# A long convolution with a routed expert layer on one core: another spacing of the indirect transfers in the plan, and new due times

## The chip, the cores and the metric

One core of a Trainium2 chip runs the kernel. The metric is the device time of one launch in microseconds (us), as the median of several runs of the same program. The engines are called PE (TensorE, matmuls), DVE (VectorE), ACT (ScalarE), POOL (GpSimd) and SP (SyncE). Here SP issues all the plain transfers, and POOL issues the indirect ones.

## The reference, cut to what matters

The first half convolves every sequence with one filter as long as the sequence. The second half sends each token to the best of eight experts.

```python
B, S, D = 8, 5696, 128            # the convolution: x (B, S, D), h (S, D)
Y = rfft(x, n=2*S, axis=1) * rfft(h, n=2*S, axis=0)[None]
y = irfft(Y, n=2*S, axis=1)[:, :S]

N, E, F = 45568, 8, 1024          # the expert layer, on y.reshape(N, D)
logits = x @ w_gate + modality_bias[modality_id]
e_idx  = argmax(logits, axis=1)
gate_w = softmax(logits)[arange(N), e_idx]
for e in range(E):
    mask = e_idx == e
    out[mask] = gate_w[mask, None] * (maximum(x[mask] @ w1[e], 0) @ w2[e])
```

## The kernel before

The transform of the convolution is cut into three passes of small matmuls with scratch tensors in device memory between them. The batch of eight is done in four groups of two (`g` = 0 to 3). `stage1` is the first pass, `stage23` multiplies by the filter in the middle, and `stage4` is the last pass together with the routing.

`stage4` goes through each group in seven chunks. For a chunk it computes the tokens (PE line 738 or 744), the logits, the best expert, and each token's place in that expert's list (`places`, DVE, which writes the tile `idx`). Then POOL sends the rows to their places: one indirect transfer for every 128 tokens (`dispatch`, line 852, `rows<-rt,idx`). There are 360 of these. A chunk's rows wait for them in the tiles `rt`, of which there are eight (`RTB`).

`experts` takes blocks of 512 tokens (256 in the last level) out of the lists: two matmuls with a ReLU between them (lines 970 to 972 and 986 to 988; `hh` on ACT at line 975 and `hl` on DVE at line 978 split each result into two parts), a turn, and the gate (DVE, line 998). Then one indirect transfer for every 128 tokens writes the result to the output (`scatter`, POOL, line 1002, `out<-of,mrt`). There are 370 of these. The first expert blocks run while later groups are still being transformed and routed; the rest run after the last dispatch.

Nothing of this stands in a fixed order of loops. Every piece is a `step` with a duration on each engine that could do it, its predecessors, the buffers that it takes and frees, and a due time. `Plan.run` plays the steps through once while the program is built, and writes the instructions of each engine in the order in which it started them there. The due times (in the table `AIMS`: knots for each stage and a lead for each kind of step) say which ready step goes first. On the chip each engine then works through its own list in order, waiting only for data and buffers; times of the plan are not in the program.

Some steps may go to either of two engines, whichever is free. For POOL those are the sum of products in `stage23` (`add`, lines 633 and 634, DVE or POOL), the rests of the splits (`low` line 640, `uu_low` line 730, lines 885 and 952) and the token numbers (`token`, line 751).

The indirect transfers have a rule of their own in the plan. A step with `lag` is an indirect transfer, 1.35 us of POOL by the plan's account. Two lines of `first` decide:

```python
apart = begun[-self.BURST[0]] + self.BURST[1 if now < AIMS["tiles"][0] else 2]
kept = now >= apart and any(r[2].lag for r in ready["POOL"])
```

`begun[-4]` is the start of the fourth indirect transfer back. Before `apart` no further one is started. While `kept` holds (a transfer is ready and may go), POOL leaves the shared steps alone. The plan's clock `now` starts at 0.0 (line 217), and the first knot of `AIMS["tiles"]` is -726 before and -550 in the change. `ROWS` is what one indirect transfer takes of the plan's transfer channel.

Of the kernel before, what the change touches and what calls it, by code (L numbers as in the profile page):

```python
# [48 lines left out]
XB = 3  # L49

AIMS = {
    "first": (None, (-605, -183, 366), (-196, 637, 137), (625, 1000, -127)),
    "over": ((-368, -101, 125), (-635, -1076, -1685), (-39, 134, -1968), (563, 670, 333)),
    "route": ((-515, -163, -633), (-1563, -310, -744), (-281, 229, 525), (795, 397, 1519)),
    "weights": (-858, 184),
    "tiles": (-726, -304, 140, 719, 198, 755, 716),
    "lead": {
# [18 lines left out]
        "experts.load": 98, "experts.load_w": -19, "experts.load_raw": -51, "experts.w_high": 137,  # L76
        "experts.w_low": -159, "experts.prep": 2, "experts.x_high": 238, "experts.x_low": -41,
        "experts.gemm1": -106, "experts.h_high": 45, "experts.h_low": -43, "experts.gemm2": 120,
        "experts.result": 10, "experts.turn": -82, "experts.gate": -153, "experts.scatter": -53,
    },  # L80
}
WP = 256
# [53 lines left out]
class Plan:  # L136
# [3 lines left out]
    SYNC = {"PE": 1.89, "DVE": 0.15, "ACT": 0.15, "POOL": 0.2, "SP": 0.1, "-": 0.0}  # L140
    LAND = 2.98
    RATE = 0.30e6
    ROWS = 58e3
    BURST = 4, 7.13, 4.97

    def __init__(self):
        self.steps = []
# [19 lines left out]
    def run(self):  # L167
# [5 lines left out]
        channel = woken = 0.0  # L173
        begun = [-100.0] * self.BURST[0]

# [22 lines left out]
        def first(e):  # L198
            nonlocal woken

            apart = begun[-self.BURST[0]] + self.BURST[1 if now < AIMS["tiles"][0] else 2]
            kept = now >= apart and any(r[2].lag for r in ready["POOL"])
# [18 lines left out]
        while True:  # L221
            for e in ready:
# [14 lines left out]
                if x.lag:  # L237
                    begun.append(now)
                    channel = max(channel, now) + self.ROWS / self.RATE
                if x.bytes:  # L240
# [954 lines left out]
```

## Time and profile before

| | before |
|---|---|
| median of 3 runs | 2449.81 us (2447.63 to 2453.53) |
| the profiled execution | 2456.72 us, of which its span is 2454.7 us |
| PE busy | 2144.5 us (87%) |
| DVE busy | 1481.0 us (60%) |
| ACT busy | 1178.3 us (48%) |
| POOL busy | 1189.2 us (48%) |
| mean granted clock of PE | 0.926 |

The span runs from the first to the last instruction. A busy share is the time in which an engine worked on an instruction, at whatever clock. The granted clock is 1.0 at full speed and 0.5 at the lower level.

### The profile page before, as it was taken

The numbers are of one execution on the slowest core, as the hardware profiler recorded it, in microseconds if no ns is written. First come the engines' busy times: TensorE is split into PE (matmuls) and PEld (weight loads), VectorE is DVE, ScalarE is ACT, GpSimd is POOL, SyncE is SP. The second block draws the span as 40 slices with busy tenths as digits, with TensorE's granted clock in tenths as the row PEclk, the third lists the DMA queues.
The fourth block names the chain that finished last, engine by engine and source line by source line (L and its number), as shares of the span: only waits on it lengthen the run. The fifth ranks groups of instructions, "written<-read, shape, count | busy, mean of one in ns | idle before, by whom it ended". The sixth has DMA issues, their size and how long they took to land.

```text
span 2454.7 us, 37648 instructions
## 1 busy us (share of the span) xinstructions
PE 2144.5 (87%) x11166; PEld 1779.7 (73%) x11166; DVE 1481.0 (60%) x2851; ACT 1178.3 (48%) x2392; POOL 1189.2 (48%) x1276
## 2 busy tenths in 40 slices
PE   5699878679775889999879889999788989999997
PEld 4578767557664667777767768887667768888897
DVE  5389645568333569975446679975354455555554
ACT  5556533335432456655445445565344344444443
POOL 2058543456445367854444566654445543333332
PEclk8899988889888999999988999999888999999999
DMA  8999887677765778964444435653323142121630
GB/s 290 292 311 322 262 260 232 219 236 234 238 183 181 221 236 260 302 226 160 145 144 142 141 106 171 203 176 105 97 72 121 58 116 74 48 78 44 248 104 26
DMA packets 236492, 434.69 MB, mean 177 GB/s; under 512 B 37318, under 2 KB 103850, under 8 KB 231681
## 3 DMA queue, kind: packets, MB, share of 16 engines
q1 hardware_dynamic: 212608, 384.15, 50.4%
q0 software_dynamic: 23680, 48.15, 5.8%
q8 instruction: 89, 1.46, 0.2%
q14 instruction: 115, 0.93, 0.1%
HBM read 408.11 MB, written 176.22 MB: 238 GB/s over the span
## 4 chain that ended last, share of the span: by engine, by line
PE 47%; issue 24%; POOL 7%; DMA 7%; another core or an unknown queue 6%; DVE 4%; ACT 2%; SPq 1%; POOLq 0%; ACTq 0%; DVEq 0%
PE bank L620 7%; POOL out L1002 4%; PE bank L972 3%; PE bank L970 3%; PE bank L552 3%; PE bank L986 3%; PE bank L971 3%; PE bank L744 3%; PE bank L987 3%; PE bank L988 3%; PE pl L763 2%; DMA zb<-z 2%; POOL rows L852 2%; DMA raw<-in_w 2%
## 5 line engine op out<-in xcount | busy, mean ns | idle before, releaser
L978 DVE SCALAR_TENSOR_TENSOR hl<-bank,hh 128x512 fp32r<-128x512 f32 x740 | 502.0, 687 | 384.8 <-ACT hh L975 239.5
L975 ACT ACTIVATE hh<-bank 128x512 fp32r<-128x512 f32 x740 | 439.3, 599 | 524.6 <-PE bank L972 309.4
L1002 POOL DMA_INDIRECT out<-of,mrt x370 | 369.0, 997 | 568.7 <-DVE of L998 425.7
L852 POOL DMA_INDIRECT rows<-rt,idx x360 | 358.7, 996 | 229.5 <-issue 127.7
L986 PE MATMUL bank<-hh,slot 128*128 128x512 f32 (+1 forms) x736 | 307.6, 418 | 22.0 <-ACT hh L975 10.9
L627 DVE TENSOR_TENSOR t<-bank,hs 96x512 f32<-96x512 f32 x418 | 264.7, 678 | 102.2 <-remote 40.0
L970 PE MATMUL bank<-mxh,slot 128*128 128x512 f32 (+1 forms) x736 | 308.2, 419 | 14.6 <-issue 8.8
L987 PE MATMUL bank<-hl,slot 128*128 128x512 f32 (+1 forms) x736 | 288.4, 392 | 2.8 <-DVE hl L978 1.7
L972 PE MATMUL bank<-mxh,slot 128*128 128x512 f32 (+1 forms) x736 | 287.7, 391 | 1.0 <-issue 1.0
L971 PE MATMUL bank<-mxl,slot 128*128 128x512 f32 (+1 forms) x736 | 287.9, 391 | 0.8 <-issue 0.7
L988 PE MATMUL bank<-hh,slot 128*128 128x512 f32 (+1 forms) x736 | 286.7, 390 | 0.6 <-issue 0.6
L620 PE MATMUL bank<-zb,m 96*96 96x256 f32 x896 | 236.3, 392 | 21.5 <-DMA zb<-z 10.8
L552 PE MATMUL bank<-xt,ft 128*128 128x256 f32 x540 | 151.8, 420 | 69.6 <-ACT z L445 27.2
L620 PEld LDWEIGHTS bank<-zb,m 96*96 96x96 f32 x896 | 146.7, 168 | 71.4 <-DVE hl L978 7.9
L445 ACT COPY ut<-bank 90x512 f32<-90x512 f32 x209 | 119.8, 581 | 132.2 <-remote 53.1
L633 POOL TENSOR_TENSOR t<-t,t 96x256 f32<-96x256 f32 x117 | 91.3, 781 | 188.7 <-DVE t L627 139.4
L986 PEld LDWEIGHTS bank<-hh,slot 128*128 128x128 f32 x736 | 143.1, 194 | 47.9 <-ACT hh L975 13.1
L970 PEld LDWEIGHTS bank<-mxh,slot 128*128 128x128 f32 x736 | 144.1, 196 | 43.9 <-issue 11.7
L552 PEld LDWEIGHTS bank<-xt,ft 128*128 128x128 f32 x540 | 108.7, 210 | 91.8 <-issue 32.0
L972 PEld LDWEIGHTS bank<-mxh,slot 128*128 128x128 f32 x736 | 142.9, 194 | 31.1 <-issue 0.8
L988 PEld LDWEIGHTS bank<-hh,slot 128*128 128x128 f32 x736 | 142.2, 193 | 29.7 <-issue 1.1
L987 PEld LDWEIGHTS bank<-hl,slot 128*128 128x128 f32 x736 | 143.1, 194 | 27.9 <-DVE hl L978 7.1
(226 smaller groups left out, 4110.3 us busy)
## 6 DMA issues: line engine op xcount, KB each, us to landing
slot<-weights SPq DMA_DIRECT2D x156, 1024.0 KB
z<-z SPq DMA_DIRECT2D x180, 256.0 KB
uu<-u SPq DMA_DIRECT2D x159, 256.0 KB
zb<-z SPq DMA_DIRECT2D x112, 360.0 KB
u<-ut SPq DMA_DIRECT2D x112, 360.0 KB
raw<-in_w SPq DMA_DIRECT2D x88, 256.0 KB
mrt<-rows SPq DMA_DIRECT2D x81, 260.0 KB
hs<-hd SPq DMA_DIRECT2D x96, 192.0 KB
```

Source lines behind the costliest of these rows:

```text
L552: nc.tensor.matmul(two(zt["ps"])[:, t], st["ft"][:, j, 2 * t:2 * t + 2, :], st["xt"][:, j], start=True, stop=True)
L620: nc.tensor.matmul(two(st["px"])[:KP, h], mm, both["zb"][:, k % 2, 1 - h], start=True, stop=True)
L852: nc.gpsimd.indirect_dma_start(views[count[0] % NVIEW], bass.IndirectOffsetOnAxis(ap=rs["idx"][:, t + c:t + c + 1], axis=0), st["rt"][:, c ...
L970: nc.tensor.matmul(po, w[0][:, fs], xh, start=True, stop=False)
L971: nc.tensor.matmul(po, w[0][:, fs], xl, start=False, stop=False)
L972: nc.tensor.matmul(po, w[1][:, fs], xh, start=False, stop=True)
L975: nc.scalar.activation(hf["hh"], hf["ph"], AF.Relu)
L978: nc.vector.scalar_tensor_tensor(hf["hl"], hf["ph"], 0.0, hf["hh"].bitcast(F32), op0=ALU.max, op1=ALU.subtract)
L986: nc.tensor.matmul(po, w[0][:, fs], hf["hh"][:, cs], start=k == 0, stop=False)
L987: nc.tensor.matmul(po, w[0][:, fs], hf["hl"][:, cs], start=False, stop=False)
L988: nc.tensor.matmul(po, w[1][:, fs], hf["hh"][:, cs], start=False, stop=k == 7)
L1002: nc.gpsimd.indirect_dma_start(oviews[(t * NSUB + c) % NVIEW], bass.IndirectOffsetOnAxis(ap=st["rt"].bitcast(I32)[:, c, D + 1:D + 2], axis=0),
```

## The change

The two gaps of `BURST`, the constant `ROWS`, and every number of `AIMS` are replaced. `AIMS["lead"]` gains entries for two kinds of steps, `fence` and `stage23.back`. No step is added or removed, and each engine's steps do the same work. The diff, with most of the table left out:

```diff
 AIMS = {
-    "first": (None, (-605, -183, 366), (-196, 637, 137), (625, 1000, -127)),
-    "over": ((-368, -101, 125), (-635, -1076, -1685), (-39, 134, -1968), (563, 670, 333)),
+    "first": (None, (-557, -190, 284), (-165, 620, 30), (608, 1003, -6)),
+    "over": ((-320, 32, 148), (-634, -1002, -1229), (148, 288, -2018), (456, 665, 85)),
...
-    "tiles": (-726, -304, 140, 719, 198, 755, 716),
+    "tiles": (-550, -95, 228, 735, -233, 786, 677),
...
-    ROWS = 58e3
-    BURST = 4, 7.13, 4.97
+    ROWS = 59e3
+    BURST = 4, 5.98, 7.06
```

The lists of POOL differ most. In both places below, a row is a line, an operation, the tile written and the tiles read, with their numbers, and how many of the same stand in a row. `L852` or `L853` (the change has one line more) are dispatches, `L1002` or `L1003` scatters.

The first place is in group 0, the dispatch of one chunk from the tiles `rt_1088` to `rt_1091`. Before:

```order
L852 DMA rows<-rt_1088,idx_1096 369152x130 x4
L852 DMA rows<-rt_1089,idx_1096 369152x130 x4
L852 DMA rows<-rt_1090,idx_1096 369152x130 x4
L852 DMA rows<-rt_1091,idx_1096 369152x130 x4
L751 COPY rt_1089<-tokid 128x4
```

With the change, the same chunk on POOL:

```order
L853 DMA rows<-rt_1088,idx_1096 369152x130 x4
L634 TENSOR_TENSOR t_1068<-t_1067,t_1068 96x256
L635 TENSOR_TENSOR t_1068<-t_1068,t_1067 96x256
L853 DMA rows<-rt_1089,idx_1096 369152x130 x4
L634 TENSOR_TENSOR t_1072<-t_1069,t_1072 96x256
L635 TENSOR_TENSOR t_1072<-t_1072,t_1069 96x256
L853 DMA rows<-rt_1090,idx_1096 369152x130 x4
L634 TENSOR_TENSOR t_1067<-t_1069,t_1067 96x256
L635 TENSOR_TENSOR t_1067<-t_1067,t_1069 96x256
L853 DMA rows<-rt_1091,idx_1096 369152x130 x4
```

One run of 16 transfers has become four runs of four, with one `add` of the other stage (two instructions) between each two.

The second place is late, in the last group, where dispatches and scatters alternate. Before, on POOL:

```order
L1002 DMA out<-of_2621,mrt_2606 45568x128 x4
L852 DMA rows<-rt_1091,idx_1096 369152x130 x3
L852 DMA rows<-rt_1090,idx_1096 369152x130 x3
L1002 DMA out<-of_2622,mrt_2607 45568x128 x4
L852 DMA rows<-rt_1090,idx_1096 369152x130
L852 DMA rows<-rt_1095,idx_1096 369152x130 x4
```

With the change, in the same part of POOL's list:

```order
L731 TENSOR_TENSOR uu_1081<-uu_1081 128x512
L853 DMA rows<-rt_1088,idx_1097 369152x130 x2
L1003 DMA out<-of_2638,mrt_2621 45568x128 x2
L752 COPY rt_1094<-tokid 128x4
L1003 DMA out<-of_2638,mrt_2621 45568x128 x2
L853 DMA rows<-rt_1088,idx_1097 369152x130 x2
L731 TENSOR_TENSOR uu_1080<-uu_1080 128x512
L853 DMA rows<-rt_1089,idx_1097 369152x130 x2
```

Here too at most four stand together, and what stands between two runs is by turns a split (line 730 before, 731 now) and a short copy of token numbers (751, now 752).

Counted over the whole list, up to the last dispatch: 45 unbroken runs of indirect transfers before, 119 now. Transfers that stand behind the eighth of their run, the last run of scatters alone left out: 280 before, 12 now. The last run, of scatters alone, has 196 transfers before and 220 now. On POOL there are 14 more `add` steps, 16 more of line 730, 16 fewer of line 640, 8 more of line 751, 4 more of line 885 and 4 fewer of line 952; the other engine that may do them has as many fewer or more. ACT takes 20 copies out of PSUM that DVE did.

## Rows read from the trace of the kernel before

**Rows 1.** Stretches: length, busy (count) of PE, PEld, DVE, ACT, POOL; clock, DMA, GB/s.

```profile
0.00:300.00 300.00, 241.74 (x1219) 200.56 (x1220) 202.86 (x324) 175.18 (x347) 139.16 (x179) 0.93 0.90 294
300.00:900.00 600.00, 476.85 (x2286) 383.94 (x2286) 304.31 (x752) 232.25 (x545) 289.83 (x315) 0.87 0.73 225
900.00:1140.00 240.00, 224.50 (x1182) 185.15 (x1180) 198.54 (x308) 147.06 (x295) 159.71 (x167) 0.96 0.79 248
1140.00:1490.00 350.00, 300.25 (x1566) 247.00 (x1565) 212.91 (x448) 164.69 (x342) 185.34 (x193) 0.90 0.45 136
1490.00:1715.00 225.00, 221.45 (x1216) 186.00 (x1215) 178.32 (x304) 128.51 (x248) 127.36 (x132) 0.99 0.54 166
1715.00:2000.00 285.00, 240.56 (x1144) 194.41 (x1143) 140.69 (x335) 116.65 (x238) 141.01 (x143) 0.89 0.30 87
2000.00:2300.00 300.00, 298.07 (x1379) 242.40 (x1378) 166.20 (x246) 144.75 (x246) 97.84 (x100) 0.99 0.28 91
```

**Rows 2.** The same stretches, instructions with tile idx alone: DVE, POOL (the dispatches).

```profile
300.00:900.00 600.00, 2.67 (x14) 179.68 (x180) 0.87 0.73 225
1140.00:1490.00 350.00, 1.27 (x7) 90.37 (x90) 0.90 0.45 136
1715.00:2000.00 285.00, 0.88 (x5) 80.77 (x82) 0.89 0.30 87
900.00:1140.00 240.00, 0.00 (x0) 0.00 (x0) 0.96 0.79 248
```

**Rows 3.** Timeline of POOL, one long run: start, duration, instruction, idle before it.

```profile
756.22 0.98 POOL L1002 DMA_INDIRECT out<-of,mrt  x1 [4.72 <-DVE of L998]
...
771.32 0.98 POOL L852 DMA_INDIRECT rows<-rt,idx  x1 [0.90 <-DVE sm L836]
...
793.46 0.98 POOL L852 DMA_INDIRECT rows<-rt,idx  x1 [0.30 <-issue]
```

**Rows 4.** The same run in stretches of 5 us, columns as in rows 1.

```profile
760.00:765.00 5.00, 5.00 (x28) 4.10 (x27) 0.52 (x2) 3.51 (x11) 3.78 (x5) 1.00 0.90 307
...
785.00:790.00 5.00, 0.00 (x0) 0.00 (x0) 0.00 (x0) 0.00 (x0) 3.78 (x5) 0.50 0.15 52
...
800.00:805.00 5.00, 5.00 (x16) 4.04 (x16) 0.00 (x0) 0.59 (x1) 0.00 (x0) 0.54 0.85 255
```

**Rows 5.** Timeline behind that run: the first ACT and PE work.

```profile
797.57 0.30 ACT L711 COPY gw<-gs 128x128 f32<-128x128 f32 x1 [16.65 <-remote]
...
799.08 2.08 PE L552 MATMUL bank<-xt,ft 128*128 128x256 f32 x4 [23.95 <-ACT z L445]
```

**Rows 6.** The run of 16 from 419.30 us, the first place of the order above.

```profile
425.00:430.00 5.00, 5.00 (x25) 3.97 (x24) 1.74 (x6) 0.59 (x1) 3.78 (x5) 1.00 0.44 155
430.00:435.00 5.00, 0.47 (x4) 0.16 (x2) 0.00 (x0) 0.00 (x0) 3.78 (x5) 0.76 0.50 137
435.00:440.00 5.00, 0.00 (x0) 0.00 (x0) 0.67 (x2) 0.00 (x0) 3.94 (x5) 0.50 0.26 92
```

**Rows 7.** Timeline of POOL: end of a run of 7, start of one of 13.

```profile
1323.13 0.98 POOL L852 DMA_INDIRECT rows<-rt,idx  x1 [0.30 <-issue]
1325.86 0.98 POOL L1002 DMA_INDIRECT out<-of,mrt  x1 [1.75 <-DVE of L998]
```

**Rows 8.** The first stretches of that run of 13, columns as in rows 1.

```profile
1326.00:1331.00 5.00, 5.00 (x31) 4.16 (x29) 5.00 (x11) 3.58 (x8) 3.78 (x4) 1.00 0.47 164
...
1336.00:1341.00 5.00, 2.44 (x11) 1.69 (x10) 1.29 (x2) 1.21 (x3) 3.92 (x4) 0.95 0.16 53
```

**Rows 9.** POOL's groups: count, busy us, mean ns, idle before them and what ended it.

```profile
L640 POOL TENSOR_TENSOR yl<-t,yh 96x512 fp32r<-96x512 f32 x76 | 99.8, 1319 | 63.4 <-ACT yh L637 57.8 <-PE bank L972 3.9 <-PE bank L988 1.4
...
L633 POOL TENSOR_TENSOR t<-t,t 96x256 f32<-96x256 f32 x117 | 91.3, 781 | 188.7 <-DVE t L627 139.4 <-DMA xt<-in_xq 40.4 <-PE bank L646 4.0
L730 POOL TENSOR_TENSOR uu<-uu 128x512 fp32r<-128x512 f32 x24 | 31.6, 1322 | 53.9 <-ACT uu L726 44.7 <-DVE yt L447 9.0
...
L751 POOL COPY rt<-tokid 128x4 int32<-128x4 int32 (+1 forms) x35 | 9.1, 278 | 0.0
```

More of the change, by code (lines that the diff above doesn't have):

```diff
@@ L51 @@
 AIMS = {
-    "first": (None, (-605, -183, 366), (-196, 637, 137), (625, 1000, -127)),
-    "over": ((-368, -101, 125), (-635, -1076, -1685), (-39, 134, -1968), (563, 670, 333)),
-    "route": ((-515, -163, -633), (-1563, -310, -744), (-281, 229, 525), (795, 397, 1519)),
-    "weights": (-858, 184),
-    "tiles": (-726, -304, 140, 719, 198, 755, 716),
-    "lead": {
[18 rows of a table removed]
[L76 to L79, printed above, removed]
+    "first": (None, (-557, -190, 284), (-165, 620, 30), (608, 1003, -6)),
+    "over": ((-320, 32, 148), (-634, -1002, -1229), (148, 288, -2018), (456, 665, 85)),
+    "route": ((-205, -198, -604), (-1533, -270, -708), (-571, 241, 527), (760, 399, 1189)),
+    "weights": (-781, 194),
+    "tiles": (-550, -95, 228, 735, -233, 786, 677),
+    "lead": {
[18 rows of a table added]
+        "fence": -108, "level.part": 21, "experts.load": 270, "experts.load_w": -54,
+        "experts.load_raw": -63, "experts.w_high": 179, "experts.w_low": -206, "experts.prep": -7,
+        "experts.x_high": 251, "experts.x_low": -11, "experts.gemm1": -160, "experts.h_high": 51,
+        "experts.h_low": -36, "experts.gemm2": 118, "experts.result": 133, "experts.turn": -88,
+        "experts.gate": -332, "experts.scatter": -44,
     },
```

36 rows, old and new, of the table AIMS are left out of this document.

## The prediction

> **What bounds the kernel now.** I read the busy time by stretch first [rows 1]. Take PE's busy time, times the granted clock, over the length of the stretch: the rate at which PE gets through its work, 1.0 at best. From 900 to 1140 us it is 224.50 x 0.96 / 240 = 0.90, from 1490 to 1715 us 221.45 x 0.99 / 225 = 0.97, and from 2000 us on 0.98. In three stretches it is lower: 476.85 x 0.87 / 600 = 0.69 from 300 to 900 us, 0.77 from 1140 to 1490 us and 0.75 from 1715 to 2000 us. No other engine is near its limit there: in the 600 us DVE works 304, ACT 232 and POOL 290. So PE waits in these stretches, and runs at a lower mean clock as well.
>
> The same stretches with only the instructions that read or write `idx` say what is special about them [rows 2]: they hold the dispatches, 180, 90 and 82 of the 360. The stretch at 0.90 has none.
>
> Then I looked at one long run of POOL. 29 indirect transfers begin at 756.22 us, and the last one begins at 793.46 us; but for one pause of 0.90 us they follow one another at 1.28 us [rows 3]. In the first 10 us PE loses nothing. From 785 to 790 us PE, ACT and DVE do nothing at all, while POOL goes on [rows 4]. The DMA engines are busy to 0.15 of their time then, so it is no lack of their time. ACT comes back at 797.57 us after 16.65 us idle, released by something that the profile does not name, and PE at 799.08 us after 23.95 us, waiting for ACT [rows 5]. Behind that PE has a clock of 0.54 for 5 us [rows 4]. The run of 16 at 419 us shows the same: ACT and DVE fall off between 425 and 430 us, PE between 430 and 435 us, at a clock that ends at the lower level, 0.50 [rows 6]. So POOL's run goes on unhurt, and about eight transfers into it the others stop.
>
> How short a run, or how long a pause, does no harm? Runs of four a tile apart, from 2000 to 2300 us, leave PE at 298 of 300 us [rows 1]. A run of 7, a pause of 1.75 us, and then a run of 13 [rows 7]: for 5 us behind that pause all three engines work well, and only 10 us into the second run PE loses half of its time [rows 8]. So 1.75 us between runs was enough there, while the 0.90 us inside the run of 29 did not prevent what came.
>
> **The change, part by part.** *The gap.* `now` starts at 0, and the first knot of `tiles` is negative before and after. So `now < AIMS["tiles"][0]` never holds, and the first of the two gaps is never used. Before, the plan asked for 4.97 us between a transfer and the fourth behind it; four of them take 4 x 1.35 = 5.4 us of the plan's POOL anyway, so there was no gap anywhere. Now it asks for 7.06 us in the whole program, a gap of 1.66 us behind each four. The "smaller one ahead of the experts", 5.98, does nothing.
>
> The gap itself is not in the program. What is there is the order: while the gap is open in the plan, `kept` is false and POOL may take a shared step. That is what the two places of the order show: an `add`, a split or a token copy behind each four. The transfers beyond the eighth of a run fall from 280 to 12, and these are the ones that see the others stop. On the chip the pause is as long as that step: an `add` is two instructions of about 0.78 us, 1.6 us in all, and the splits are 1.32 us, with an idle time ahead of them of 188.7 / 117 = 1.6 us for the first and 63.4 / 76 = 0.8 us for the one at line 640 [rows 9]. With it the pause is 2 to 3 us, over the 1.75 us above. A token copy gives 0.28 us, which is below the 0.90 us that was too short.
>
> *What it can give.* If the three stretches ran at the same 0.898, their work of 415, 270 and 214 us (busy time by clock, rows 1) would take 462, 301 and 239 us: 138, 49 and 46 less. The first cannot have all of it, because its transfers would have to fit: 0.73 x 600 = 438 us of DMA time. At the share of 0.90 of the first 300 us that takes 487 us, 113 less; at the 0.79 of the stretch at 0.90 it takes 554 us, 46 less. I take 80, the middle. The sum is 80 + 49 + 46 = 175 us. Of the late 46 us I keep half, 23: there the pause is by turns only a token copy. Of the other 129 us I keep 0.7, 90: the order all but ends the long runs, but a pause of 1.3 to 1.6 us lies close below the one that I know to be enough, where the step's data are ready. Together 113 us. The bounds are 0 (no pause is long enough) and 138 + 49 + 46 = 233 us (all of it, and the transfers keep up).
>
> In rows 4 ACT stops while nothing but POOL's transfers goes on. The Trainium skill's page "SBUF — State Buffer", section "Who interferes with whom", speaks against any such gain: transfers never contend with a compute engine, and PE and ACT never wait for anyone there. By that rule a run of transfers stops nothing, the term of 113 us is 0, and the sum is the 2450 us of before. The trace does not agree, as far as rows 4 go, and I give the rule the chance of rival three.
>
> *The moved work.* POOL gets 14 more `add` steps, 14 x 1.6 = 22 us. The 16 more of line 730 and the 16 fewer of line 640 cancel, at 1.32 us each [rows 9]; the rest are a few us. POOL is busy for 0.48 of the span and DVE is relieved, so I count nothing. Without that cover it would be the 22 us.
>
> *The due times.* They reorder all engines' lists. I see one thing in them that can be checked: the last run of scatters has 196 transfers before and 220 now, so 24 more come behind the last dispatch. From 2000 to 2300 us there were 100 [rows 1], 3.0 us each: 72 us more of expert work at the end, at full rate. It isn't a cost; it is work that no longer fills waits earlier. Where the rest moves a wait I can't tell, and I leave it at nothing, with rival two as its price.
>
> **The sum.** 2456.7 - 113 = 2343.6 us for a profiled execution. The one shown lies 6.9 us above the median of its runs, so 2336.7 us; I say 2337.
>
> **The rivals.**
>
> *One: the pauses are too short.* Four transfers, 5.1 us, and a step of 1.3 to 1.6 us stay below the 7.06 us that the plan asks for, and the trace has no case of many runs of four so close together. If a pause only delays the stop, a fifth of the 113 us is left: 2427 us. Against it stand rows 7 and 8, and the steps' own waits.
>
> *Two: slower, POOL's list becomes the bound.* POOL works in order. A shared step between two runs waits for its own data, and all transfers behind it wait too; then the eight `rt` tiles stay taken, and `stage4` on PE stops. For the first 180 dispatches the order has 11 runs before and 43 now, 32 more pauses, nearly all of them from 300 to 900 us. POOL is busy for 290 of the 600 us there, and the 0.30 us ahead of each of the 180 dispatches makes another 54 [rows 1 to 3]: 256 us are free. At the 1.6 us of rows 9 the new pauses take 51 of them. From 8 us each POOL is full; from 10.5 us each, (256 + 80) / 32, the loss is larger than the 80 us that the stretch may gain. At 12 us it is 48 us over that; the other two stretches give 0.7 x 49 + 23 = 57 us, and if half of that is lost in the same way, 28 us remain: 2450 + 48 - 28 = 2470 us. Waits of that kind exist: the first chain in rows 9 waits for DVE's products, which themselves wait for PE.
>
> *Three: no change, the runs are not the cause.* Dispatches come with chunks whose results everybody waits for; then the number of transfers, 730 as before, is what counts and not their spacing. That gives about 2450 us. For it: ACT's releaser in rows 5 is unnamed. Against it: the engines stop at the same place in the run in rows 4, 6 and 8, and none stops in the first 5 us. The Trainium skill's rule above, of the page "SBUF — State Buffer", would have it so.
>
> **How the numbers follow.** A difference of 0.2%, 4.9 us, is about what can be told from no change here. The forecast has a chance of 0.59, rival one 0.20, rival two 0.13, rival three 0.08. Faster are the forecast, most of rival one (0.17) and a little of rival three (0.02): 0.78. Same are 0.02 of rival one and 0.04 of rival three: 0.06. Slower are rival two and what is left of the others: 0.16. The forecast's own range is 2270 (all of the 175 us) to 2400 us (50 us gained). The range of 8 in 10 goes from 2255 us, a little below the 175 us towards the bound of 233, up to 2450 us: it leaves out rival two and the far tails.
>
> **What would show it.** Right: POOL's timeline has runs of four with a shared step between them; PE's waits of over 10 us between 300 and 900 us are gone; the rate of that stretch rises from 0.69 to about 0.8 with a DMA share of about 0.85; the mean clock rises above 0.93; and the last dispatch, before 2000 us until now, comes at about 2000 - 113 - 72 = 1815 us. Rival one: the same order, but ACT and DVE still idle in a series of runs. Rival two: POOL waits long at lines 634, 641 or 731, and PE for `rt`. Rival three: PE waits as long, at the same chunks, whatever the runs. What would make the forecast wrong above all is that the last two stretches keep their waits, because the short pauses of the late part stand behind those of 1140 to 1490 us as well.

## The result, and the profile after

The changed kernel takes 2284.57 us (median of 4 runs, 2280.05 to 2290.42). The kernel before, beside it on the same chip, took 2448.72 us (4 runs, 2438.36 to 2453.53). The ratio is 0.934, with a 95% interval of 0.930 to 0.938: 164 us faster, where 113 were forecast. The profiled execution took 2281.1 us with a span of 2279.3 us and a mean granted clock of 0.952. PE is busy for 2089.6 us (92%) and POOL for 1218.5 us (53%).

That is the result on one chip. The experiments ran on chips on which the kernel before took other times, 2166 to 2171 us on three and 2470 us on one. The next section shows that this decides what the change is worth. The chip of the first comparison isn't named; by its times it is of the second kind.

The stretches of the kernel after, columns as in rows 1, to be laid beside [rows 1]:

```profile
300.00:900.00 600.00, 522.27 (x2621) 427.42 (x2619) 372.55 (x841) 275.84 (x633) 348.46 (x385) 0.91 0.84 259
900.00:1140.00 240.00, 229.99 (x1264) 192.58 (x1264) 177.30 (x304) 150.80 (x321) 153.92 (x161) 0.98 0.74 237
1140.00:1490.00 350.00, 342.81 (x1906) 289.11 (x1905) 291.94 (x521) 202.45 (x392) 245.45 (x258) 0.99 0.56 166
1490.00:1715.00 225.00, 211.45 (x1159) 174.53 (x1158) 131.06 (x285) 117.41 (x250) 132.08 (x134) 0.98 0.36 113
1715.00:2000.00 285.00, 274.42 (x1258) 221.15 (x1257) 158.23 (x292) 129.64 (x225) 113.47 (x117) 0.98 0.27 78
```

PE's work in a stretch (busy time by clock) rises from 415 to 475 us between 300 and 900 us, from 270 to 339 between 1140 and 1490, and from 214 to 269 between 1715 and 2000. In the two stretches between it goes from 216 to 225 and from 219 to 207. Work done earlier is time saved at the end: 60 + 69 + 55 + 9 - 12 = 181 us, of which the first 300 us take back 5 (225 before; 220 after). The two spans lie 175 us apart. The medians lie 164 apart, because the profiled execution of before is 8.0 us above the median of its runs and that of after 3.5 us below.

POOL's timeline after, around 470 us, and its dispatches as a whole (count, duration in ns, first and last start):

```profile
462.86 1.05 POOL L853 DMA_INDIRECT rows<-rt,idx  x1 [0.30 <-issue]
467.09 0.72 POOL L634 TENSOR_TENSOR t<-t,t 96x256 f32<-96x256 f32 x1 [3.18 <-DVE t L628]
467.78 0.72 POOL L635 TENSOR_TENSOR t<-t,t 96x256 f32<-96x256 f32 x1
468.66 0.99 POOL L853 DMA_INDIRECT rows<-rt,idx  x1 [0.16 <-issue]
...
472.76 0.97 POOL L853 DMA_INDIRECT rows<-rt,idx  x1 [0.30 <-issue]
473.75 0.75 POOL L634 TENSOR_TENSOR t<-t,t 96x256 f32<-96x256 f32 x1
474.43 0.94 POOL L635 TENSOR_TENSOR t<-t,t 96x256 f32<-96x256 f32 x1
475.53 0.99 POOL L853 DMA_INDIRECT rows<-rt,idx  x1 [0.16 <-ACT ex L813]
```
```profile
L853 POOL DMA_INDIRECT rows<-rt,idx x360: 968/978/1827, 369.5 to 1812.7; - x180
```

The same line of the kernel before:

```profile
L852 POOL DMA_INDIRECT rows<-rt,idx x360: 969/980/1566, 327.6 to 1986.1; - x180
```

Four transfers, an `add`, four transfers: between two fours lie 4.75 us (463.91 to 468.66) and 1.80 us (473.73 to 475.53). The last dispatch starts at 1812.7 us; before it was 1986.1.

Not every run of transfers is broken. One of 12 is left at 699 us; POOL's timeline of its first and last transfer, and then the stretches of 5 us, columns as in rows 1:

```profile
699.27 1.41 POOL L853 DMA_INDIRECT rows<-rt,idx  x1 [0.16 <-issue]
...
714.26 0.97 POOL L853 DMA_INDIRECT rows<-rt,idx  x1 [0.30 <-issue]
```
```profile
702.00:707.00 5.00, 4.49 (x24) 3.74 (x25) 3.37 (x9) 1.98 (x6) 3.82 (x4) 1.00 0.86 231
707.00:712.00 5.00, 1.06 (x5) 0.56 (x3) 3.01 (x11) 1.60 (x3) 3.78 (x5) 1.00 0.88 268
712.00:717.00 5.00, 0.00 (x0) 0.00 (x0) 0.00 (x0) 0.35 (x2) 2.62 (x3) 0.55 0.97 248
717.00:722.00 5.00, 3.31 (x10) 2.67 (x11) 1.96 (x4) 3.32 (x8) 0.00 (x0) 0.50 1.03 329
```

It does what the long runs of [rows 4, 6] did: from 712 to 717 us PE and DVE do nothing, and the clock falls to the lower level. Here the DMA engines are busy to 0.97 meanwhile, where it was 0.15 in rows 4, so the stop goes neither with little traffic alone nor with much. The three longest waits of PE behind 300 us are of this kind; its waits (us in all, times, longest):

```profile
PE bank L647 <- issue: 12.0, 2, 10.0
...
PE bank L757 <- ACT rt L446: 10.6, 1, 10.6
PE bank L757 <- issue: 9.9, 2, 9.5
```

The one of 10.0 stands in a run of 24 (405 us), that of 9.5 in a run of 16 (665 us), that of 10.6 in the run of 12.

### The profile page after: what moved, and what is told of

It is laid out like the page before. It is cut to its first block, busy times and chain, and to the rows that moved or that the text cites. A ratio compares the mean times of both kernels' runs of the same rounds, so it can differ in the third digit from the quotient of the medians.

```text
span 2279.3 us, 37642 instructions
## 1 busy us (share of the span) xinstructions
PE 2089.6 (92%) x11166; PEld 1748.0 (77%) x11166; DVE 1476.4 (65%) x2795; ACT 1185.1 (52%) x2412; POOL 1218.5 (53%) x1312
## 5 line engine op out<-in xcount | busy, mean ns | idle before, releaser
L1003 POOL DMA_INDIRECT out<-of,mrt x370 | 367.1, 992 | 448.0 <-DVE of L999 346.5
L853 POOL DMA_INDIRECT rows<-rt,idx x360 | 367.1, 1020 | 115.8 <-issue 96.5
L987 PE MATMUL bank<-hh,slot 128*128 128x512 f32 (+1 forms) x736 | 302.9, 411 | 6.2 <-ACT hh L976 4.5
L971 PE MATMUL bank<-mxh,slot 128*128 128x512 f32 (+1 forms) x736 | 301.1, 409 | 3.6 <-DVE z L448 2.2
L973 PE MATMUL bank<-mxh,slot 128*128 128x512 f32 (+1 forms) x736 | 283.7, 386 | 0.3 <-issue 0.3
L989 PE MATMUL bank<-hh,slot 128*128 128x512 f32 (+1 forms) x736 | 283.6, 385 | 0.0
L634 POOL TENSOR_TENSOR t<-t,t 96x256 f32<-96x256 f32 x134 | 108.5, 810 | 185.0 <-DVE t L628 117.7
L971 PEld LDWEIGHTS bank<-mxh,slot 128*128 128x128 f32 x736 | 141.2, 192 | 29.7 <-DVE z L448 2.6
L973 PEld LDWEIGHTS bank<-mxh,slot 128*128 128x128 f32 x736 | 140.4, 191 | 29.9 <-issue 0.4
L972 PEld LDWEIGHTS bank<-mxl,slot 128*128 128x128 f32 x736 | 141.3, 192 | 23.4 <-issue 0.3
```

Of the source, the lines that this page charges most:

```text
L853: nc.gpsimd.indirect_dma_start(views[count[0] % NVIEW], bass.IndirectOffsetOnAxis(ap=rs["idx"][:, t + c:t + c + 1], axis=0), st["rt"][:, c ...
L971: nc.tensor.matmul(po, w[0][:, fs], xh, start=True, stop=False)
L972: nc.tensor.matmul(po, w[0][:, fs], xl, start=False, stop=False)
L973: nc.tensor.matmul(po, w[1][:, fs], xh, start=False, stop=True)
L987: nc.tensor.matmul(po, w[0][:, fs], hf["hh"][:, cs], start=k == 0, stop=False)
L989: nc.tensor.matmul(po, w[1][:, fs], hf["hh"][:, cs], start=False, stop=k == 7)
```

## The experiments

Theory: a run of indirect transfers on POOL stops ACT, DVE and then PE, and what counts is how many follow one another without a pause. Its rivals are those of the prediction: the runs are not the cause, or POOL's list becomes the bound. All runs of one group below stand beside runs of the kernel before on their own chip.

**First group (chip 5): the gap, and pauses without another order.** `gap_alone` keeps the due times of before and takes only the second gap, 105 runs of transfers in place of 45:

```diff
-    BURST = 4, 7.13, 4.97
+    BURST = 4, 7.13, 7.06
```

> The due times of before, with the second gap alone set from 4.97 to 7.06 us. The order then has 105 runs of indirect transfers instead of 45, and 62 transfers behind the eighth of their run instead of 280 (12 with the whole change). If the runs are the cause (my theory), most of the change's 164 us come with this: 2310 to 2360 us. If the new due times are the cause, this stays within 20 us of before, 2430 to 2460 us.

`pause_before` keeps the order of before on every engine, and adds memsets of a small tile to POOL's list behind every fourth transfer of a run:

```diff
                 x.emit(e)
+                if x.lag:
+                    self.row += 1
+                    if self.row == 4:
+                        self.pause()
+                        self.row = 0
+                elif e == "POOL" and x.work[e] > 0.8:
+                    self.row = 0
...
+    def pause():
+        for _ in range(12):
+            nc.gpsimd.memset(idle, 0.0)
+    plan.pause = pause
```

A step of POOL of over 0.8 us, by the plan's account, starts the count of four anew.

> The order of before on every engine, with 12 short memsets on POOL (some 1.6 us, a tile that nobody reads) behind each fourth indirect transfer of a run. Nothing else moves, and POOL does more, not less. If the runs are the cause: PE's waits inside runs go, 2310 to 2370 us. If due times or the moved work are the cause: 2450 us or more, because POOL only loses time. If the number of transfers counts and not their spacing: 2450 us or more, too.

`pause_before_short` has 3 memsets for the 12, `pause_after` puts the 12 into the kernel after.

> As pause_before, with 3 memsets (some 0.4 us) in place of 12. If a pause has to last about 1.75 us, as the trace of before suggests, a tenth to a third of the gain of pause_before: 2400 to 2445 us. If any POOL instruction between the transfers breaks the run, whatever its length, as much as pause_before or more: under 2370 us.

> The changed kernel, with the same 12 memsets where four indirect transfers follow one another with no shared step of over 0.8 us between them. If the rest of the runs (24, 16, 16, 12 and 12 long in its trace) still costs PE its waits of about 10 us each, some 20 to 40 us less than the changed kernel: 2245 to 2265 us. If the pauses only delay dispatches: 2285 us or more.

Measured: every one of them took longer than before, and the kernel before took 2166.39 us on this chip (7 runs, 2161.38 to 2174.78).

| | median us | ratio to before (95%) |
|---|---|---|
| gap_alone | 2224.31 | 1.026 (1.023 to 1.030) |
| pause_before | 2373.67 | 1.095 (1.091 to 1.099) |
| pause_before_short | 2199.53 | 1.015 (1.012 to 1.018) |
| pause_after | 2321.16 | 1.072 (1.068 to 1.076) |

My expectations rested on a kernel before of 2449 us. Either the theory was wrong, or this chip has no stop that a pause could take away. Here a pause only costs POOL's time.

**Second group (chip 8): both kernels again.** The same kernels once more, to get a trace of each on such a chip.

> The changed kernel once more, beside runs of the kernel before on the same chip. So far the kernel before took 2449 us where the two were first compared, and 2166 us on the chip of the four runs above, 283 us less. Theory one: these 283 us are the stop of the engines in long runs of indirect transfers, which one chip has and the other not. Then the changed kernel, with 12 transfers left behind the eighth of a run where the kernel before has 280, takes nearly the same time on both: on a chip where the kernel before takes about 2166 it takes 2285 - 283 x 12/280 = about 2270 (between 2230 and 2290), 5% slower than before; where the kernel before takes about 2449 it is again 0.93 of it. Rival: the chips differ by a factor for all work (2449 / 2166 = 1.13), and the order gains the same share on both: 0.93 on either, 2021 us where before takes 2166.

> The kernel before, for its trace. Where it takes about 2166 us, theory one expects TensorE idle less than 40 us between 300 and 700 us (72.2 in [rows 2]'s run) and no stop in the long runs: ScalarE and VectorE go on beside the ninth and later transfer of a run. The rival expects the same stops, shorter by a factor 1.13. Where it takes about 2449 us, both expect the trace of before as it was.

> The second gap alone, again: before's due times, 7.06 for 4.97. It leaves 62 of 280 transfers behind the eighth of a run. Theory one: on a chip where the kernel before takes about 2449 us it takes 2224 + 283 x 62/280 = 2287 us (2250 to 2350), 0.92 to 0.96 of before; where before takes 2166, 1.026 again. Rival (what it costs is the same share on every chip): 1.026 on either, 2513 us where before takes 2449.

> Before's order unchanged, with 12 memsets (about 2.1 us) behind every fourth transfer of a run, again. Theory one: no run goes on for more than four, so its time is that on the other chip, 2374 us (2340 to 2400), wherever it runs: 0.97 of before where before takes 2449, 1.095 where before takes 2166. Rival (the pauses only cost GpSimd's time): 1.095 on either, 2682 us where before takes 2449.

Measured: before 2169.87 us (17 runs), after 2177.16 (ratio 1.004, 1.002 to 1.005), gap_alone 2224.83 (1.026, 1.024 to 1.029), pause_before 2379.91 (1.097, 1.095 to 1.100). So on this chip the change gains nothing; it costs 7 us. Theory one had expected 2270 us for the kernel after, and its rival 2021; both missed. For the trace of before, theory one was right: PE is idle for 14.7 us between 300 and 700 us, where under 40 were expected and the first chip had 72.2. The traces say what differs. The kernel before in stretches, columns as in rows 1:

```profile
300.00:900.00 600.00, 564.52 (x2934) 463.19 (x2934) 432.58 (x935) 321.06 (x718) 397.69 (x422) 0.97 0.91 285
...
1140.00:1490.00 350.00, 346.83 (x1918) 292.04 (x1916) 291.25 (x522) 199.60 (x384) 227.06 (x233) 1.00 0.54 165
...
1715.00:2000.00 285.00, 278.98 (x1286) 226.94 (x1285) 155.99 (x230) 135.89 (x230) 89.90 (x92) 0.99 0.25 79
```

The rates are 0.91, 0.99 and 0.97, where [rows 1] give 0.69, 0.77 and 0.75 for the same program. And a run of 28 transfers from 608.9 to 645.8 us in stretches of 5 us:

```profile
610.00:615.00 5.00, 5.00 (x31) 4.39 (x30) 2.97 (x8) 3.08 (x9) 3.89 (x4) 1.00 0.71 215
...
625.00:630.00 5.00, 5.00 (x26) 4.29 (x25) 3.15 (x5) 4.12 (x12) 3.94 (x4) 1.00 0.95 295
...
640.00:645.00 5.00, 5.00 (x30) 4.22 (x29) 1.98 (x4) 3.16 (x10) 3.78 (x5) 1.00 1.01 351
```

Nothing stops; compare the run of 29 in [rows 4]. POOL issues at the same pace on both. The busy share of the other engines in the 1.3 us from the start of a transfer, by its place in the run (runs end at a pause of 1 us), as means over all 730 transfers of a trace:

```
place in      before, first chip      before, chip 8         after, first chip      after, chip 8
the run        n   PE  ACT  DVE       n   PE  ACT  DVE       n   PE  ACT  DVE       n   PE  ACT  DVE
1-4          416  .99  .45  .59     344  .98  .46  .59     572  .97  .49  .67     581  .97  .52  .68
5-6           74  .98  .35  .37      47 1.00  .58  .70      58  .99  .40  .46      57 1.00  .62  .53
7-8           65  .84  .20  .30      46 1.00  .66  .71      53  .91  .19  .21      51  .97  .60  .60
9-10          58  .52  .18  .18      44  .98  .57  .75      17  .66  .13  .28      17  .89  .55  .54
11 and on    117  .37  .10  .18     249  .97  .55  .67      30  .33  .10  .09      24 1.00  .57  .61
```

On the first chip all depends on the place in the run, in both kernels. ACT and DVE are down well ahead of the eighth transfer, in the kernel before at five and six already (0.35 and 0.37, where chip 8 has 0.58 and 0.70). On chip 8 no engine falls off with the place. That also says why the kernel after was not 2270 us here: theory one allowed the stop only what lies behind the eighth, 12 us by the expectation, and it costs that kernel 107.

**Third group (chip 5, then chip 1): a break behind the eighth, and the fourth once more.** `pause_before_8` has `self.row == 8` in the edit above.

> Before's order with the 12 memsets behind every eighth transfer of a run, where pause_before had them behind every fourth. The pauses cost GpSimd's time: with about half as many, about half of the 207 us of pause_before, so 2270 us where the kernel before takes about 2167 (2225 to 2310, 1.03 to 1.07 of before). Theory (on a chip where before takes about 2449 us, long runs stop the other engines, and a break behind the eighth ends the stop): there 2270 plus the 107 us that the changed kernel, with most of its runs at eight or fewer, still loses between the two chips, about 2375 us, 0.97 of before (2320 to 2430). Rival (the stop has another cause than a run's length): 1.05 of before there too, about 2570 us.

> The pause behind every fourth transfer once more (before's order, 12 memsets). Theory: no run is longer than four, so it takes about 2375 us on every chip (2340 to 2420), 0.97 of before where the kernel before takes about 2449 us, 1.096 where it takes about 2170. Rival (the stop has another cause than a run's length): 1.096 on either, about 2685 us where before takes 2449.

Measured: pause_before_8 2222.70 us beside 2171.11 (1.025, 1.022 to 1.029); pause_before_third 2378.87 beside 2168.22 (1.097, 1.092 to 1.102). Neither chip has the stop. pause_before_8 says only that 77 pauses (924 memsets) in place of 181 (2172) cost a quarter, 52 us for the 207 to 211, where I had expected about half (2225 to 2310 us).

**Fourth group (chip 12): the stop is there.** The last two runs came to a chip on which the kernel before takes 2469.65 us (3 runs, 2464.68 to 2470.1).

> The pause behind every fourth transfer (before's order), in case the kernel before takes about 2449 us on this chip. Theory: 2375 us on every chip, 0.97 of before there. Rival: 1.096 of before on every chip.

> The second gap alone (before's due times), in case the kernel before takes about 2449 us on this chip. Theory: 0.92 to 0.97 of before there, 1.026 where before takes about 2170. Rival: 1.026 on every chip.

Measured: pause_before 2380.67 us (2 runs), 0.965 of before (0.962 to 0.967); gap_alone 2358.56 us (2 runs), 0.956 (0.946 to 0.965). The rival's 1.096 and 1.026 are excluded; 2375 us for pause_before was right within 6 us, and gap_alone lies in the 0.92 to 0.97 expected. Stretches of pause_before, columns as in rows 1, first on chip 12 and then on chip 1:

```profile
300.00:900.00 600.00, 499.82 (x2456) 403.95 (x2456) 336.87 (x799) 255.67 (x591) 401.37 (x989) 0.90 0.78 242
...
1140.00:1490.00 350.00, 311.40 (x1686) 263.45 (x1685) 236.11 (x487) 177.11 (x357) 257.89 (x624) 0.92 0.50 151
```
```profile
300.00:900.00 600.00, 500.22 (x2442) 402.97 (x2442) 329.02 (x797) 255.03 (x588) 400.53 (x987) 0.90 0.77 240
...
1140.00:1490.00 350.00, 309.14 (x1691) 260.96 (x1690) 237.59 (x489) 175.91 (x356) 257.92 (x626) 0.94 0.49 151
```

They are the same but for a few us, and so is the time of the whole. Nor is a stop hidden behind the pauses: in the 1.3 us from the start of a transfer PE, ACT and DVE are busy to 0.89, 0.48 and 0.57 on chip 12 and to 0.89, 0.49 and 0.56 on chip 1. With no run longer than four the two kinds of chip no longer differ; so the 300 us between them (2469.65 and 2168.22 for the kernel before) come with the long runs. Each break is short, as POOL's timeline on chip 12 shows: 2.85 us from the end of a fourth transfer (351.12) to the next.

```profile
350.14 0.98 POOL L861 DMA_INDIRECT rows<-rt,idx  x1 [0.30 <-issue]
351.10 2.16 POOL L1120 MEMSET idle<- 128x32 f32 x12
353.97 0.98 POOL L861 DMA_INDIRECT rows<-rt,idx  x1 [0.71 <-ACT ut L454]
```

All kernels that ran on both kinds, with what the stop costs each:

| | without the stop | with the stop | the stop |
|---|---|---|---|
| before | 2166 to 2171 | 2449, 2470 | 279 to 300 |
| gap_alone | 2224.8 | 2358.6 | 134 |
| after | 2177.2 | 2284.6 | 107 |
| pause_before | 2373.7 to 2379.9 | 2380.7 | 1 to 7 |

The second column joins two chips, the first one (before 2449, and after) and chip 12 (before 2470, and the two variants), so its rows can be compared to within some 20 us. The short pauses, the break behind the eighth and `pause_after` ran only where there is no stop. How short a pause may be, and whether a break behind the eighth is enough, is therefore not shown.

The pauses' own price, 207 to 211 us without the stop, is for about half rival two's mechanism: PE waits for products of POOL that stand behind transfers and pauses. The four longest groups of PE's waits in pause_before on chip 8 (us in all, times, longest), and the longest of the kind in before there:

```profile
PE bank L655 <- POOL t L643: 30.5, 5, 10.0
PE bank L659 <- ACT yh L646: 27.9, 2, 27.2
PE bank L661 <- POOL yl L649: 27.0, 9, 15.2
PE bank L753 <- POOL uu L739: 26.5, 4, 10.1
```
```profile
PE bank L646 <- POOL t L634: 6.5, 1, 6.5
```

The four come to 112 us. The second belongs to them by ACT's timeline, where ACT itself waits for POOL's sum, which stands behind ten transfers and three pauses:

```profile
853.24 0.62 ACT L646 CAST yh<-t 96x512 fp32r<-96x512 f32 x1 [27.88 <-POOL t L643]
```

And gap_alone's price without the stop, 55 us, is for the larger part one wait: PE for rows of the expert lists, from 1753 to 1787 us, around the last dispatch, which starts at 1764.1 us there, 1698.6 in before and 1704.7 in after. From gap_alone on chip 8, then from before and after there:

```profile
PE bank L956 <- DMA mrt<-rows: 35.2, 4, 33.9
```
```profile
PE bank L956 <- DMA mrt<-rows: 6.6, 2, 6.0
```
```profile
PE bank L957 <- DMA mrt<-rows: 9.4, 3, 6.3
```

The due times alone, without the gap, have no run: with the gap at 4.97 the plan with the new due times comes to steps that wait for each other. That the first of the two gaps is without effect needs no run: with 99.0 for 5.98 the program stays the same.

## Why the prediction was right

*The place of the loss.* Right, and more so than I thought. The three stretches hold the dispatches, and without the stop the same program runs through them at 0.91, 0.99 and 0.97.

*The cause.* Right for chips with the stop: the order of before, with nothing but pauses, gains 89 us on chip 12 and takes the same time on both kinds of chip. That there are chips without the stop, and that this one has it, the prediction did not ask; on chip 8 the forecast would have failed, with 7 us lost. Rival three (the number of transfers counts, not their spacing) falls by that: the 730 transfers and all other work are the same, and only the pauses differ. The rule on page "SBUF — State Buffer", section "Who interferes with whom", in the Trainium skill would have transfers never hold up a compute engine. The traces of chips 5 and 8 agree with it, those of the first chip and chip 12 do not: PE is busy for 0.97 of the time on chip 8 (before), 0.37 on the first (before) and 0.24 on chip 12 (gap_alone) from the eleventh transfer of a run on. Which of the two a chip does can't be read from the program, and whether the stop has to do with the SBUF at all, no run here shows.

*How short a run.* "About eight transfers into it the others stop" was late for ACT and DVE, which fall from the fifth on and are down at the seventh (0.19 and 0.21, after, first chip), and right for PE (0.66 at nine and ten). Pauses of 1 to 2 us do no harm, as rows 7 and 8 said of one of 1.75 us: the places one to four are alike on both chips, and the 61 of them that stand behind such a pause in the kernel after, on the first chip, have PE at 0.95, ACT at 0.56 and DVE at 0.79. The token copy was too short, as I feared: in the run of 16 at 655 us three copies of 0.2 us stand. The order was said to leave 12 transfers behind an eighth, but on the chip 47 come ninth or later in a run without a pause of 1 us, 175 before. Rival one is true of these alone. 107 us are left to the stop, of which 71 lie between 300 and 900 us (475 us of PE's work there; 546 on chip 8 by the rows below).

*The sum.* Here the size was off. By the work that PE gets done in each stretch, the terms of 80, 49 and 46 us were 60, 69 and 55: 184 in place of 175. The first was too large, and not for the reason that I gave, the room for its transfers: without the stop the kernel after does 131 us more of work in that stretch than before did with it, at a DMA share of 0.92 (chip 8). What is missing went into the stop, with the runs of 24, 16 and 12 that are left there. The other two were too small, since 0.898, the rate of the stretch at 900 us, was no ceiling: without the stop that stretch has 0.98 itself (chip 8, after). The step that failed is the discount from 175 to 113 us: 0.7 of the first two terms and half of the last. Together the three came in full, the late one with 55 for 46 although only token copies were to stand there by turns; the stretches between and the first 300 us took back 8. The rates of the kernel after without the stop, columns as in rows 1:

```profile
300.00:900.00 600.00, 563.19 (x2938) 464.53 (x2937) 436.64 (x927) 317.96 (x712) 397.10 (x434) 0.97 0.92 288
900.00:1140.00 240.00, 235.06 (x1364) 200.78 (x1363) 184.80 (x339) 157.13 (x334) 159.42 (x164) 1.00 0.69 220
```

*Moved work and due times, both at nothing.* Nearly right in their sum, and wrong apart. Without the stop the gap costs 55 us by itself; with the new due times the two cost 7 us. So these give back 48 us; the last dispatch comes 59 us earlier with them. In the comparison forecast, 279 - 107 = 172 us of the stop go and 7 us are paid: 165. That this meets the 164 measured proves nothing, because the three figures are differences of the same four times. One reading of the order was wrong: the last unbroken run is not of scatters alone. In the traces it holds 26 dispatches before and 36 after, and behind the last dispatch come 154 scatters before and 150 after. So the 72 us of more expert work at the end do not exist: from the last dispatch to the end are 468.6 us before and 466.6 after. The counts of transfers behind an eighth, 280 and 12, leave those dispatches out too.

The counts of the moved work are as the order had them: 162 `add` steps for 148 over all their forms, and 40 of the split of line 730, now 731, for 24. Its group after (count, busy us, mean ns, idle before), to be laid beside [rows 9]:

```profile
L731 POOL TENSOR_TENSOR uu<-uu 128x512 fp32r<-128x512 f32 x40 | 52.7, 1327 | 96.0 <-ACT uu L727 71.7 <-DMA z<-z 17.2 <-PE bank L973 2.7
```

*Rival two.* It did not come: POOL is busy for 348 of the 600 us, and its products hold PE up by 6.4 us at line 647 and 5.3 us at line 653. Its mechanism is real, as pause_before shows with 112 us.

*What would show it.* Of the signs named: runs of four with a shared step, seen; rate 0.79 for "about 0.8", with a DMA share of 0.84 for 0.85; mean clock 0.952 for "above 0.93"; last dispatch at 1812.7 for 1815 us. The last is luck: it moved by 173 us from 1986.1, where the sum took 113 and the 72 that do not exist from 2000. "Waits of over 10 us gone" failed: one of 10.6 and one of 10.0 us are left.

## What to carry to other kernels

Long unbroken runs of indirect transfers on GpSimd can go with a stop of PE, ACT and DVE, on some chips; keep them at four or so with some 2 us of other GpSimd work between, and take for that work which is there anyway: empty pauses gave 89 us on a chip with the stop and cost 207 to 211 on one without, while shared steps with due times to match gave 164 and cost 7. A stop that the trace gives no releaser for may belong to the chip and not to the program, so time such a change on several chips before counting on its gain. Price a change of spacing where its queue ends, not only where the gap lies: the gap's own cost came from the last dispatch, some 1400 us behind the first of the gaps (332 us on chip 8).

## What was not expected of the hardware

The stop goes with the chip: for one program 2166 to 2171 us on chips 1, 5 and 8, and 2470 us on chip 12, of which only chip 5 was used at two times. Why is open. One thing goes with it: the traces with the stop hold fewer records of semaphore events, 29,368 for 42,875 in the kernel before (first chip; chip 8), which may be why [rows 5] name no releaser. The loss sets in with the first indirect transfers, at 327.6 us: the two traces of before hold 1738 and 1719 such records from 240 to 320 us, and 862 and 2376 from 320 to 400 us. `pause_before` loses them too, 32,952 on chip 12 for 45,124 on chip 1, in equal time, so their loss costs nothing by itself. Every time here was taken with a recorded span, so no run shows whether the recording has a part in the stop; that rival stays open. The stop also lowers the clock: over the whole program the mean is 0.926 for before on the first chip and 0.975 on chip 8.
